# Attention into a gated MLP block: two casts ahead of the power on GpSimd, one cast later, a key turn moved, one output row to ScalarE, four stores to GpSimd's queue

## The chip, the core and the metric

The kernel runs on one core of one Trainium2 chip. The core has five engines that run their own instruction streams side by side and wait for each other through semaphores: TensorE (PE; its weight loads are listed apart as PEld), VectorE (DVE), ScalarE (ACT), GpSimd (POOL) and SyncE (SP), which here does nothing but start DMA transfers. ACT and POOL can start transfers as well; a letter q behind a name (SPq, POOLq) means the part of an engine that starts them. The metric is the device time of one execution in microseconds (us), as the median over several runs.

## What is computed

Attention over 4 batches, 8 heads, 768 positions and 64 features, in which each position sees the 128 latest positions and 4 "sink" positions at the start; then a block on the result `x` (768 x 512 for each batch):

```python
scores = scale * q @ k.T                       # kept where is_sink or in_window
a = exp(scores - max) / (sum + 1e-09)
x = (a @ v), heads side by side                # (4, 768, 512)

h = gelu_tanh(x @ w_in)                        # (768, 1024)
u, v = h[..., :512], h[..., 512:]
v_n = (v - mean(v)) / sqrt(var(v) + 1e-06) * g_ln
v_s = einsum('ts,bsd->btd', w_sg, v_n) + b_sg  # mixes positions
out = x + (u * v_s) @ w_out
```

## The kernel before

**Pairs.** Two heads of a batch are one pair `n`; batch b has the pairs 4b to 4b+3, so pairs 0 to 15 in all. "Pair 11" below is the pair with n = 11, the twelfth. For each pair:

- `load_all(n)` starts on SP the loads of k and q of pair n and of v of pair n-1; each kind has three buffers.
- `cast(n, which, G)` makes bf16 of them on POOL (L108 for k and q, L105 for v). k_bf and q_bf have two buffers each, v has four.
- `columns` turns k and q on PE, six 128x128 transposes into a PSUM bank (L221), and copies the result to SBUF on ACT (L225) or DVE (L227). `columns_by_dma` (L235) does it with two transposing DMAs on SP instead.
- `score(n, groups)` makes the scores of three groups (L269, L279) and takes the exponential on ACT (L283). `keep_band` puts zeros outside the window: group 0 on DVE (L292), groups 1 and 2 on POOL, two instructions each (L300, L302).
- `values(n, 0)` and `values(n, 1)` multiply with v (L326, L332) and divide on DVE (L334, L335) into `x_sb`. `turn_x` (L343, L352) or `turn_x_by_dma` (L356) turns x.

**Batches.** When four pairs are done, `hidden(b)` runs: six units `hidden_v` (L372, L379, gelu on ACT at L381, mean and variance on DVE at L383 and L384), eight units `hidden_u` (L391, L394). After the second of the latter comes `inverse_root`: `w`, variance plus epsilon, on DVE (L406), and its power -1/2, `y`, on POOL (L407). Then six `normalise` on DVE (L413), each reading fp32 from SBUF and writing bf16.

**Fillers.** The rest of a batch's work is put into a list of small units, which are mixed into the next batch's pairs so that PE always has something to do: eight `spatial` (six matmuls at L423, then two DVE instructions, L426 and L429) and six `project` (one for each 128 rows: four matmuls at L455). A row ends in one of two ways: DVE adds x to the PSUM bank and writes `o_sb` (L465), or PE adds x with one more matmul by the identity (L458) and ACT copies (L463). Then a store leaves (L467), on SP unless `store` says otherwise; `o_sb` has six buffers. The last row of the last batch goes in two halves (`project_last`, L440 to L447), one by DVE and SP, one by ACT and its own queue.

**Order.** Nothing is scheduled by a program: each engine's instructions stand in the order in which the text issues them, and an engine that waits holds up everything behind it in its own stream. The text of `ORDER` and `INSIDE` spells the order of steps for pairs 4 to 15. `S n g` is `score`, `m n g` is `keep_band`, `A0`/`A1` is `values`, `ck`/`cq`/`cv` are the casts on POOL, `KA`/`QA`/`QV` is `columns` with the copy on ACT or DVE, `TD` is `columns_by_dma`, `XV`/`XD` turns x, `L` is `load_all`, `F 1` takes one filler, `B b` runs `hidden(b)`. `INSIDE[b]` names steps between the units of `hidden(b)`: step i stands behind unit i, units 0 to 5 being `hidden_v` and 6 to 13 `hidden_u`; the power is issued behind unit 7.

**Limits on running ahead.** `bank` hands out four PSUM banks in turn to all of `columns`, `values`, `turn_x`, `hidden_*`, `spatial` and `project`, so PE can be at most four such units ahead of the engine that empties them; scores have two double banks of their own.

At the end of the kernel, the sixteen pairs' reciprocals are checked on POOL and PE, each engine reads the count, and a branch that is hardly ever taken follows.

Of the kernel before, what the change touches and what calls it, by code (L numbers as in the profile page):

```python
# [18 lines left out]
def kernel(  # L19
# [14 lines left out]
    nc = tc.nc  # L34
    V, G, A = nc.vector, nc.gpsimd, nc.scalar

    B, H, S, Dh = q.shape
# [10 lines left out]
    HT = NT // 2  # L48
# [162 lines left out]
    def bank(shape, dtype, name):  # L211
        return ps_m.tile(shape, dtype, name=name, tag="m")
# [162 lines left out]
    def hidden_v(b, j):  # L375
        if (b, j) not in hvs:
            open_v(b, j)
        h_ps, c = hvs.pop((b, j)), KD - 1
        nc.tensor.matmul(h_ps, xT[b][:, c, 128 * j:128 * (j + 1)],  # L379
                         w_in_sb[:, c, DF:], start=False, stop=True)  # L380
        A.activation(out=v_alls[b][:, j, :], in_=h_ps, func=AF.Gelu_apprx_tanh)  # L381
        st = small.tile([128, 6], F32, name="st")
        V.bn_stats(out=st, in_=v_alls[b][:, j, :])  # L383
        V.bn_aggr(out=mvs[b][:, j, :], in_=st)  # L384

    def hidden_u(b, f, n):
        if f == 0 and n == 0:
            uTs[b] = work.tile([128, KU, S], BF16, name="uT", bufs=1)
        h_ps = bank([128, 512], F32, "hu")
        for c in range(KD):  # L390
            nc.tensor.matmul(h_ps[:, 0:NH], w_in_sb[:, c, 128 * f:128 * (f + 1)],  # L391
                             xT[b][:, c, NH * n:NH * (n + 1)],
                             start=(c == 0), stop=(c == KD - 1))
        A.activation(out=uTs[b][:, f, NH * n:NH * (n + 1)],  # L394
                     in_=h_ps[:, 0:NH], func=AF.Gelu_apprx_tanh)
# [6 lines left out]
    def inverse_root(b):  # L402

        w = small.tile([128, NT], F32, name="w", bufs=2)
        y = small.tile([128, NT], F32, name="y", bufs=2)
        V.tensor_scalar(out=w, in0=mvs[b][:, :, 1], scalar1=1e-6, scalar2=None, op0=ALU.add)  # L406
        G.tensor_tensor(out=y, in0=w, in1=minus_half, op=ALU.pow)  # L407
        rstds[b] = y

    def normalise(b, j):  # L410
        if j == 0:
            vns[b] = work.tile([128, NT, DF], BF16, name="vn", bufs=1)
        V.tensor_scalar(out=vns[b][:, j, :], in0=v_alls[b][:, j, :],  # L413
                        scalar1=mvs[b][:, j, 0:1], scalar2=rstds[b][:, j:j + 1],
                        op0=ALU.subtract, op1=ALU.mult)

    def spatial(b, f, n):
        if f == 0 and n == 0:
            gTs[b] = work.tile([128, KU, S], BF16, name="gT", bufs=1)
        cols = slice(NH * n, NH * (n + 1))  # L420
        vs = bank([128, 512], F32, "vs")
        for si in range(NT):
            nc.tensor.matmul(vs[:, 0:NH], vns[b][:, si, 128 * f:128 * (f + 1)],  # L423
                             wsgT[:, si, cols], start=(si == 0), stop=(si == NT - 1))
        gv = small.tile([128, NH], BF16, name="gv")
        V.scalar_tensor_tensor(  # L426
            out=gv, in0=vs[:, 0:NH], scalar=g_sb[:, f:f + 1], in1=b_bc[:, cols],
            op0=ALU.mult, op1=ALU.add)
        V.tensor_mul(gTs[b][:, f, cols], gv, uTs[b][:, f, cols])  # L429
# [19 lines left out]
    def project(b, t, by_act, ends=None, store=nc.sync):  # L449

        rows = slice(128 * t, 128 * (t + 1))
        o_ps = bank([128, 512], F32, "o_ps")
        o_sb = small.tile([128, DM], F32, name="o_sb", bufs=6)
        for c in range(KU):
            nc.tensor.matmul(o_ps, gTs[b][:, c, rows], w_out_sb[:, c, :],  # L455
                             start=(c == 0), stop=(c == KU - 1 and not by_act))
        if by_act:
            nc.tensor.matmul(o_ps.rearrange("p (h d) -> p h d", h=HP), iden, x_sb[b][:, :, t, :],  # L458
                             start=False, stop=True)

        def end():
            if by_act:
                A.copy(o_sb, o_ps)  # L463
            else:
                V.tensor_add(o_sb.rearrange("p (h d) -> p h d", h=HP),  # L465
                             o_ps.rearrange("p (h d) -> p h d", h=HP), x_sb[b][:, :, t, :])
            store.dma_start(out=out[b, rows, :], in_=o_sb)  # L467

        if ends is None:
            end()  # L470
        else:
            ends.append(end)
# [107 lines left out]
    fillers = []  # L580
# [6 lines left out]
    def hidden(b, between):  # L587
        units = [lambda j=j: hidden_v(b, j) for j in range(NT)]
        units += [lambda f=f, n=n: hidden_u(b, f, n) for n in range(2) for f in range(KU)]
        after = {NT + 1: [lambda: inverse_root(b)]}  # L590
        for j in range(NT):
            after.setdefault(NT + 1 + j, []).append(lambda j=j: normalise(b, j))
        for i, unit in enumerate(units):
            unit()
            for step in after.get(i, []) + between.get(i, []):
                step()
        gate = [[lambda f=f, n=n: spatial(b, f, n) for f in range(KU)] for n in range(2)]
        if b < B - 1:
            fillers.extend(gate[0] + gate[1])
            by_act = (1,)  # L600
            order = (0, 2, 4, 1, 3, 5) if b < B - 2 else (1, 0, 2, 3, 4, 5)
            fillers.extend(lambda ends=None, t=t: project(b, t, t in by_act, ends) for t in order)
            return


        rows = [lambda t=t: project(b, t, t in (0, 4), store=nc.sync if t else G)
                for t in range(NT - 1)]
        fillers.extend(gate[0] + [gate[1][0], rows[0], gate[1][1], gate[1][2], rows[1],
                                  gate[1][3]] + rows[2:])
        fillers.append(lambda: project_last(b, NT - 1))  # L610
# [85 lines left out]
    for j in range(3):  # L696
# [15 lines left out]

    LAST = NT + 2 * KU - 1
    INSIDE = {
        1: {1: "A0 8", 3: "A1 8", 5: "KA 9", 6: "L 12", 7: "QA 9",
            9: "XD 8, ck 11, cq 11, TD 11, L 13", LAST: "cv 10, S 9 0 1, F 1, QV 10, F 1"},
        2: {1: "A0 12", 3: "A1 12", 6: "L 15, L 16", 9: "XD 12", LAST: "S 13 0 1, F 2"},
    }
    ORDER = """
        S 4 0 1, W 3 4 5, m 4 0 1, F 1, KA 5, QV 5, F 1, S 4 2, m 4 2, ck 6, cq 6, cv 5, F 1,  # L720
        L 8, S 5 0 1, A0 4, m 5 0 1, F 1, KA 6, S 5 2, m 5 2, A1 4, F 1, QA 6,
        ck 7, cq 7, cv 6, F 1, XV 4,
        L 9, S 6 0 1, A0 5, m 6 0 1, F 1, KA 7, S 6 2, m 6 2, A1 5, F 1, QA 7,
        ck 8, cq 8, cv 7, F 1, XV 5,
# [1 line left out]
        ck 9, cq 9, cv 8, F 1, XV 6,  # L726
        L 11, S 8 0 1, A0 7, m 8 1, D, S 8 2, m 8 2, A1 7, E, m 8 0, ck 10, cq 10, cv 9,
        O 1 0, O 1 1, XV 7, O 1 2, B 1,
        m 9 0 1, F 1, KA 10, F 1, S 9 2, m 9 2, ck 12, cq 12, TD 12, F 1,
        S 10 0 1, A0 9, m 10 0 1, F 1, S 10 2, m 10 2, A1 9, XD 9, L 14,  # L730
        F 1, cv 11, ck 13, cq 13, TD 13, F 1,
        S 11 0 1, A0 10, m 11 0 1, F 1, S 11 2, m 11 2, A1 10, F 1, cv 12, ck 14, cq 14, TD 14,
# [8 lines left out]
    ends = []  # L741
# [97 lines left out]
```

## Time and profile before

| | |
|---|---|
| median of 3 runs | 164.02 us (163.75 to 164.38) |
| the profiled execution, its own time | 164.03 us |
| its span in the trace | 162.0 us |
| DMA, mean over the span | 196 GB/s, 31.68 MB |
| stores of output rows on SP, 256 KB each | 22 |
| store of an output row on POOL | 1 |

The span runs from the first to the last instruction in the trace; some 2 us of the execution's own time lie outside of it. A row of the timeline gives start, length, engine, line, operation, what is written from what, how many instructions were merged, and in brackets how long the engine had been idle before and what released it. Consecutive matmuls overlap in the profile's model, so the start of the next one tells more about PE's pace than the length of one. In answers by stretches the columns are: the stretch, its length, busy time (and number of instructions) of each engine, the clock granted to PE, the DMA engines' share, and GB/s.

### The profile page before, as it was taken

The page shows a single profiled execution, that of the slowest core. Times are in us where ns is not written, and L with a number is a line of the kernel's source. Part 1 is how long each engine was busy: PE and PEld are TensorE (multiplying, and loading weights), DVE is VectorE, ACT ScalarE, POOL GpSimd, SP SyncE. Part 2 cuts the span into 40 slices and gives each one's busy share as a digit, 9 for nine tenths or more (in the row PEclk, how much of TensorE's full clock was granted, in tenths as well). Part 3 has the DMA queues.
Part 4 walks back from the last instruction along what each step waited for, and adds up shares of the span by engine and source line. Part 5 has one row for each costly group of instructions (what it writes and reads, how often), then busy time and mean ns, then how long its engine had stood idle before and what let it go on. Part 6 is the DMA issues. An engine that isn't in the chain of part 4 may idle for free.

```text
span 162.0 us, 4332 instructions
## 1 busy us (share of the span) xinstructions
PE 150.3 (93%) x1713; PEld 89.9 (55%) x1731; DVE 128.8 (79%) x279; ACT 103.0 (64%) x139; POOL 87.2 (54%) x121
## 2 busy tenths in 40 slices
PE   2999999999999999999899999999999899999940
PEld 2546574566667675565556655565566445555420
DVE  6786985966899995796999994969999957797820
ACT  3179978789777699788865576679659157401020
POOL 6567680434899989708449997031997221101000
PEclk9999999999999999999999999999999999999995
DMA  4999979999999999999897999999626420050352
GB/s 129 339 337 264 210 103 272 222 254 318 305 232 321 260 304 314 234 256 171 182 249 175 154 220 126 304 236 200 178 52 53 134 109 4 0 194 0 129 202 75
DMA packets 65090, 31.68 MB, mean 196 GB/s; under 512 B 53829, under 2 KB 62041, under 8 KB 65065
## 3 DMA queue, kind: packets, MB, share of 16 engines
q1 hardware_dynamic: 61616, 27.80, 74.8%
q0 software_dynamic: 3024, 3.03, 11.0%
q10 hardware_dynamic: 424, 0.53, 1.0%
q8 instruction: 15, 0.25, 0.7%
q14 instruction: 11, 0.08, 0.1%
HBM read 24.81 MB, written 6.29 MB: 192 GB/s over the span
## 4 chain that ended last, share of the span: by engine, by line
PE 45%; DVE 23%; issue 11%; POOL 10%; DMA 3%; ACT 3%; SPq 1%; POOLq 0%; ACTq 0%; DVEq 0%
PE vs L423 9%; PE hu L391 7%; PE o_ps L455 6%; PE hv L372 5%; DVE gv L426 4%; DVE gT L429 4%; DVE vn L413 4%; PE sc L269 3%; PE av L326 3%; DMA q_sb<-in_q_dram 3%; ACT ex L283 2%; DVE x L335 2%; POOL ex L300 2%; POOL ex L302 2%; PE kps L221 2%
## 5 line engine op out<-in xcount | busy, mean ns | idle before, releaser
L283 ACT ACTIVATE ex<-sc 128x1024 bf16<-128x1024 f32 x48 | 47.5, 1024 | 15.3 <-PE sc L269 6.4
L423 PE MATMUL vs<-wsgT,vn 128*128 128x384 bf16 x192 | 35.3, 326 | 0.5 <-DVE qT L227 0.4
L423 PEld LDWEIGHTS <-vn 128*128 128x128 bf16 x192 | 17.9, 98 | 11.3 <-issue 0.5
L300 POOL TENSOR_SCALAR_AFFINE_SELECT ex<-ex 128x512 bf16<-128x512 bf16 x24 | 18.6, 773 | 10.4 <-ACT ex L283 10.4
L455 PE MATMUL o_ps<-w_out_sb,gT 128*128 128x512 bf16 x83 | 22.2, 379 | 0.9 <-DVE x L335 0.4
L391 PE MATMUL hu<-xT,w_in_sb 128*128 128x384 bf16 x128 | 22.4, 326 | 0.0
L426 DVE SCALAR_TENSOR_TENSOR gv<-vs,g_sb,b_bc 128x384 bf16<-128x384 f32 x32 | 19.5, 610 | 2.1 <-PE vs L423 1.4
L381 ACT ACTIVATE v_all<-hv 128x512 f32<-128x512 f32 x24 | 13.3, 599 | 9.6 <-PE hv L379 8.4
L383 DVE BATCH_NORM_STATS2 st<-v_all 128x6 f32<-128x512 f32 x24 | 16.1, 670 | 3.5 <-ACT v_all L381 3.5
L335 DVE TENSOR_TENSOR x<-av,rcps 128x384 bf16<-128x384 f32 x32 | 17.8, 557 | 1.1
L372 PE MATMUL hv<-w_in_sb,xT 128*128 128x512 bf16 x68 | 18.4, 379 | 0.3
L394 ACT ACTIVATE uT<-hu 128x384 bf16<-128x384 f32 x32 | 15.7, 493 | 4.3 <-PE hu L391 3.8
L108 POOL CAST k_bf<-k_sb 128x768 bf16<-128x768 f32 x15 | 12.7, 845 | 10.3 <-DMA k_sb<-in_k_dram 10.3
L413 DVE TENSOR_SCALAR vn<-v_all,mv,y 128x512 bf16<-128x512 f32 x24 | 13.3, 619 | 5.9 <-POOL y L407 5.9
L429 DVE TENSOR_TENSOR gT<-gv,uT 128x384 bf16<-128x384 bf16 x32 | 15.5, 484 | 1.9
L108 POOL CAST q_bf<-q_sb 128x768 bf16<-128x768 f32 x15 | 14.7, 981 | 3.3 <-DMA q_sb<-in_q_dram 2.4
L391 PEld LDWEIGHTS <-w_in_sb 128*128 128x128 bf16 x128 | 12.1, 98 | 7.7
L269 PE MATMUL sc<-qT,kT 64*128 64x256 bf16 (+2 forms) x384 | 16.0, 256 | 0.4
L407 POOL TENSOR_TENSOR y<-w,minus_half 128x6 f32<-128x6 f32 x4 | 5.4, 1345 | 20.0 <-DVE w L406 20.0
L326 PE MATMUL av<-v_sb,ex 128*128 128x65 bf16 x352 | 16.1, 194 | 0.0
L326 PEld LDWEIGHTS <-ex 128*128 128x128 bf16 x352 | 13.0, 97 | 4.9 <-issue 1.7
L105 POOL CAST v_sb<-v_sb 128x768 bf16<-128x768 f32 x16 | 13.7, 855 | 3.4 <-DMA v_sb<-in_v_dram 3.3
(89 smaller groups left out, 216.5 us busy)
## 6 DMA issues: line engine op xcount, KB each, us to landing
k_sb<-in_k_dram SPq DMA_DIRECT2D x16, 384.0 KB, 6.9
v_sb<-in_v_dram SPq DMA_DIRECT2D x16, 384.0 KB, 6.4
q_sb<-in_q_dram SPq DMA_DIRECT2D x15, 384.0 KB, 6.9
out_dram<-o_sb SPq DMA_DIRECT2D x22, 256.0 KB, 2.6
wsg_sb<-in_moe_w_sg_dram POOLq DMA_DIRECT2D x2, 576.0 KB, 11.4
w_in_sb<-in_moe_w_in_dram POOLq DMA_DIRECT2D x2, 256.0 KB, 5.8
w_in_sb<-in_moe_w_in_dram POOLq DMA_DIRECT2D x1, 512.0 KB, 6.7
w_out_sb<-in_moe_w_out_dram POOLq DMA_DIRECT2D x1, 512.0 KB, 9.5
```

What stands on the lines that cost most here:

```text
L108: eng.tensor_copy(dst.rearrange("p t (h d) -> p h t d", h=2), src)
L269: nc.tensor.matmul(sc[part, 512 * l + w:512 * l + w + n_q], kT[rows, 128 * j + wide * a:128 * j + wide * (a + 1)], qT[rows, 128 * j:128 * ...
L283: A.activation(out=exps[n][:, g, :], in_=sc, func=AF.Exp, scale=scale)
L300: eng.affine_select(out=diag, in_=diag, compare_op=ALU.is_ge, fill=0.0, base=0, pattern=[[0, 2], [0, 2], [1, 128]], channel_multiplier=-1)
L326: nc.tensor.matmul(av[:, m, l, :], probs(j, l, half), v_sb[:, l, j, :], start=first, stop=False)
L335: V.tensor_mul(x_sb[b][:, hp, HT * c:HT * (c + 1), :].rearrange("p i (l d) -> p i l d", l=2), av[:, :, :, 0:64], rcp.to_broadcast([128, HT ...
L372: nc.tensor.matmul(hvs[b, j], xT[b][:, c, 128 * j:128 * (j + 1)], w_in_sb[:, c, DF:], start=(c == 0), stop=False)
L391: nc.tensor.matmul(h_ps[:, 0:NH], w_in_sb[:, c, 128 * f:128 * (f + 1)], xT[b][:, c, NH * n:NH * (n + 1)], start=(c == 0), stop=(c == KD - 1))
L423: nc.tensor.matmul(vs[:, 0:NH], vns[b][:, si, 128 * f:128 * (f + 1)], wsgT[:, si, cols], start=(si == 0), stop=(si == NT - 1))
L426: V.scalar_tensor_tensor(out=gv, in0=vs[:, 0:NH], scalar=g_sb[:, f:f + 1], in1=b_bc[:, cols], op0=ALU.mult, op1=ALU.add)
L429: V.tensor_mul(gTs[b][:, f, cols], gv, uTs[b][:, f, cols])
L455: nc.tensor.matmul(o_ps, gTs[b][:, c, rows], w_out_sb[:, c, :], start=(c == 0), stop=(c == KU - 1 and not by_act))
```

## The change

Four edits in the order of work; no instruction's work changes but for one output row that ends on another engine.

1. `ck 11` and `cq 11` move in `INSIDE[1]` from step 9 to step 6, which is ahead of the power (behind unit 7) in POOL's stream. `cv 10` moves from the end of `hidden(1)` into `ORDER`, behind `ck 12, cq 12`. `TD 11`, which reads the first two, stays at step 9.
2. `KA 6` moves behind `S 5 2, m 5 2`.
3. For the batch `B - 3`, which is batch 1, row 5 ends by ACT as row 1 does.
4. For the batch `B - 2`, which is batch 2, the last three rows in its order (3, 4 and 5) are stored by POOL; of the last batch row 3 (`HT`) is stored by POOL and row 0 by SP.

```diff
         if b < B - 1:
             fillers.extend(gate[0] + gate[1])
-            by_act = (1,)
+            by_act = (1, 5) if b == B - 3 else (1,)
             order = (0, 2, 4, 1, 3, 5) if b < B - 2 else (1, 0, 2, 3, 4, 5)
-            fillers.extend(lambda ends=None, t=t: project(b, t, t in by_act, ends) for t in order)
+
+            by_pool = () if b < B - 2 else order[-3:]
+            fillers.extend(lambda ends=None, t=t: project(b, t, t in by_act, ends,
+                                                          G if t in by_pool else nc.sync)
+                           for t in order)
             return
...
-        rows = [lambda t=t: project(b, t, t in (0, 4), store=nc.sync if t else G)
+        rows = [lambda t=t: project(b, t, t in (0, 4), store=G if t == HT else nc.sync)
                 for t in range(NT - 1)]
...
     INSIDE = {
-        1: {1: "A0 8", 3: "A1 8", 5: "KA 9", 6: "L 12", 7: "QA 9",
-            9: "XD 8, ck 11, cq 11, TD 11, L 13", LAST: "cv 10, S 9 0 1, F 1, QV 10, F 1"},
+        1: {1: "A0 8", 3: "A1 8", 5: "KA 9", 6: "L 12, ck 11, cq 11", 7: "QA 9",
+            9: "XD 8, TD 11, L 13", LAST: "S 9 0 1, F 1, QV 10, F 1"},
...
-        L 8, S 5 0 1, A0 4, m 5 0 1, F 1, KA 6, S 5 2, m 5 2, A1 4, F 1, QA 6,
+        L 8, S 5 0 1, A0 4, m 5 0 1, F 1, S 5 2, m 5 2, KA 6, A1 4, F 1, QA 6,
...
-        m 9 0 1, F 1, KA 10, F 1, S 9 2, m 9 2, ck 12, cq 12, TD 12, F 1,
+        m 9 0 1, F 1, KA 10, F 1, S 9 2, m 9 2, ck 12, cq 12, TD 12, cv 10, F 1,
```

## The prediction

> **What bounds the kernel now.** I read the page first (engines, chain), then the busy time by stretch, then the timeline of each engine round the places that the diff touches.
>
> ```profile
> span 162.0 us, 4332 instructions
> PE 150.3 (93%) x1713; PEld 89.9 (55%) x1731; DVE 128.8 (79%) x279; ACT 103.0 (64%) x139; POOL 87.2 (54%) x121
> ...
> PE 45%; DVE 23%; issue 11%; POOL 10%; DMA 3%; ACT 3%; SPq 1%; POOLq 0%; ACTq 0%; DVEq 0%
> ```
>
> TensorE (PE) is nearly always busy, so a stage gets shorter only where PE really waits. The chain nevertheless spends a third of its time on VectorE (DVE) and GpSimd (POOL): there are stretches in which PE keeps pace with DVE instead of running ahead. In the answer by stretches the second column is the length, and then come PE, PEld, DVE, ACT and POOL:
>
> ```profile
> 76.00:80.50 4.50, 4.08 (x33) 2.29 (x31) 4.50 (x8) 3.91 (x5) 2.10 (x4) 1.00 0.76 157
> 80.50:98.00 17.50, 17.33 (x262) 10.26 (x264) 17.01 (x38) 10.37 (x11) 15.18 (x21) 1.00 1.14 204
> ...
> 112.00:128.40 16.40, 15.91 (x227) 9.59 (x227) 15.95 (x35) 10.58 (x12) 11.00 (x15) 1.00 0.53 96
> ```
>
> From 76 to 80.5 DVE has no free moment (4.50 of 4.50) and PE does (4.08); from 112 to 128.4 DVE is as full as PE (15.95 and 15.91 of 16.40). Those two places can yield time. The granted clock (the column after POOL) is 1.00 in all of them, so it plays no part.
>
> **Part 1: the casts of pair 11 ahead of the power, the v cast of pair 10 later.** Around the second batch's power `y`:
>
> ```profile
> 71.55 0.50 PE L221 MATMUL qps<-iden,q_bf 128*128 128x128 bf16 x6
> ...
> 73.34 1.34 POOL L407 TENSOR_TENSOR y<-w,minus_half 128x6 f32<-128x6 f32 x1 [5.34 <-DVE w L406]
> ...
> 74.66 0.81 POOL L108 CAST k_bf<-k_sb 128x768 bf16<-128x768 f32 x1
> ...
> 76.39 1.02 POOL L105 CAST v_sb<-v_sb 128x768 bf16<-128x768 f32 x1
> ```
>
> POOL stands idle for 5.34 us before `y`, and then runs three casts from 74.66 to 77.41, exactly while DVE normalises (L413, six instructions). The same six instructions in the three batches (length, then DVE's busy time in them alone):
>
> ```profile
> 73.30:79.10 5.80, 4.33 (x6) 1.00 0.97 168
> 107.80:112.60 4.80, 3.31 (x6) 1.00 1.38 218
> 137.10:141.50 4.40, 2.88 (x6) 1.00 0.00 0
> ```
>
> Three casts beside them: 4.33 us; one cast (the third batch): 3.31; none: 2.88. That is 0.43 to 0.48 us of DVE per cast, and 1.45 us in all for batch 1. The change takes all three away from there.
>
> What do they cost where they go? The k and q casts (0.81 and up to 1.35, the longest cast quoted below) fall into the idle 5.34 us. The q cast overwrites one of two buffers, and in the new order it comes before the query turn of pair 9 in the text, so it must wait for that turn's transposes on PE (71.55 plus 0.50, 72.05). It then ends at 72.9 to 73.4, and `w` releases `y` at 73.34. So `y` keeps its place or slips by 0.1 at most; behind it in POOL's queue stand the masks of pair 9, which wait for ScalarE anyway. Nothing is lost even if `y` slipped by 1 us, since the normalisation behind it is 1.45 us shorter. The moved casts issue no DMA. Behind them on SP stand the two transposing DMAs of pair 11, which become free earlier, and the loads of pair 14, whose v buffer this cast now releases at 87 or so (behind the q cast of 85.26, quoted under B) instead of at 77.41; it is asked for at 91.51:
>
> ```profile
> 91.51 1.67 SPq L96 DMA_DIRECT2D v_sb<-in_v_dram  x1
> ```
>
>
> What does PE gain? At present:
>
> ```profile
> 78.50 1.14 PE L423 MATMUL vs<-wsgT,vn 128*128 128x384 bf16 x6
> ...
> 80.56 1.14 PE L423 MATMUL vs<-wsgT,vn 128*128 128x384 bf16 x6 [0.37 <-DVE qT L227]
> 81.63 0.36 PE L269 MATMUL sc<-qT,kT 64*32 64x256 bf16 x16
> ```
>
> The two units and the key turn between them take 81.63 - 78.50 = 3.13 us. Unhindered ones are in the next fence: a turn from 47.84 to 48.17 (0.33) and a unit from 48.17 to 49.15 (0.98). So 0.98 + 0.33 + 0.98 = 2.29, and PE loses 0.84 here to DVE's late normalisation and the copies queued behind it. With DVE 1.45 earlier all of that goes: **-0.85**. Its bounds are 0 (the wait returns further on, rival B) and -1.45 (DVE's whole lead, were DVE the only limit).
>
> **Part 2: pair 6's key turn behind the scores of pair 5, third group.**
>
> ```profile
> 44.34 1.14 PE L423 MATMUL vs<-wsgT,vn 128*128 128x384 bf16 x6
> 45.53 0.51 PE L221 MATMUL kps<-iden,k_bf 128*128 128x128 bf16 x6
> 45.97 0.36 PE L269 MATMUL sc<-qT,kT 64*32 64x256 bf16 x16
> ...
> 46.32 0.54 PE L326 MATMUL av<-v_sb,ex 128*128 128x65 bf16 x12
> ...
> 47.84 0.50 PE L221 MATMUL qps<-iden,q_bf 128*128 128x128 bf16 x6
> 48.17 1.14 PE L423 MATMUL vs<-wsgT,vn 128*128 128x384 bf16 x6
> 49.15 0.50 PE L343 MATMUL xps<-iden,x 128*128 128x128 bf16 x6
> ```
>
> The unit at 44.34 is through at 45.32; the turn starts at 45.53, waiting for POOL's cast. With the scores (0.35) first, the turn runs from 45.67 to 46.00, and `av` starts 0.32 earlier. On ScalarE the key copy now stands behind one more exponential (1.02 in the row of 114.55 below), and a unit that reuses the copy's bank comes just after it, so a little may be given back. I take **-0.25**, between 0 and -0.32.
>
> **Part 3: row 5 of the second batch ends on ScalarE.** DVE loses one of two additions, PE gains one identity matmul, ScalarE one copy.
>
> ```profile
> 112.43 1.27 DVE L465 TENSOR_TENSOR o_sb<-o_ps,x 128x512 f32<-128x512 f32 x2
> 113.64 1.16 POOL L300 TENSOR_SCALAR_AFFINE_SELECT ex<-ex 128x512 bf16<-128x512 bf16 x1 [3.70 <-ACT ex L283]
> 114.55 1.02 ACT L283 ACTIVATE ex<-sc 128x1024 bf16<-128x1024 f32 x1 [0.99 <-PE sc L279]
> ...
> 120.40 0.33 PEld L269 LDWEIGHTS <-kT 64*128 64x128 bf16 x8 [0.32 <-issue]
> ...
> 126.31 0.55 PEld L455 LDWEIGHTS <-gT 128*128 128x128 bf16 x4 [0.56 <-DVE x L335]
> ```
> ```profile
> 148.07 0.22 PE o_ps L458
> ```
>
> DVE is 1.27/2 = 0.63 us lighter at the start of the stretch in which it is full, and at the end of that stretch PE waits 0.56 for DVE. The wait goes; the extra matmul costs 0.22, partly inside time that PE spends on the normalisation anyway. The copy fits into ScalarE's idle 0.99. The row's store stands ahead of pair 15's transposes on SP and leaves about half a us later; pair 15's scores need them at 120.40. Net -0.56 + 0.22 = **-0.35**; bounds +0.22 and -0.56.
>
> **Part 4: the four stores on GpSimd's queue.** Rows 3, 4, 5 of the third batch leave while PE works on the last batch's gates; behind them SP and POOL only read the count for the branch at the very end. Row 0 of the last batch returns to SP. What matters is row 3 of the last batch. The first row is SP's issue just before its last one; the line of the DMA engines cuts 154 to 162 us into 40 slices; then the length of SP's 22 issues (min/median/max in ns) and, over all stores, the time from issue to landing, and the same for the one store that POOL issues now:
>
> ```profile
> 155.53 1.12 SPq L467 DMA_DIRECT2D out_dram<-o_sb  x1
> ```
> ```profile
> DMA  0009997989400102999989971110000000100000
> ```
> ```profile
> L467 SPq DMA_DIRECT2D out_dram<-o_sb x22: 332/373/1677, 56.9 to 155.5; - x22
> ...
> DMA to landing us min/median/max: 2.1/2.5/3.9
> ```
> ```profile
> DMA to landing us min/median/max: 2.4/2.4/2.4
> ```
>
> SP's last issue, the last half row, stands behind this one of 1.12 us. Were that as short as the shortest, 0.33, the last store could be issued 0.79 earlier, with row 3 out of SP's queue. But the DMA line says what the end waits for: after 158.6 only a tenth of the engines still works, and the slowest store needs 3.9 us against 2.1. One or two late DMA engines finish last, and moving row 3 to another queue does not take its bytes off them. POOL's landing of 2.4 keeps row 3 ahead of the last store. I take **0**, with -0.79 and +0.3 (2.4 against 2.1, if row 3 were last) as bounds. The Trainium skill says the same in "DMA: Bandwidth & Descriptors", section "Issuing engines are not separate DMA queues": DMAs from all engines run on the same 16 engines, and spreading them only saves issue time. By that rule at most the 0.79 could come.
>
> **The sum.** -0.85 - 0.25 - 0.35 + 0 = -1.45. The profiled execution took 164.03 us (span 162.0, 2.0 around it), the median of the runs is 164.02: 164.03 - 1.45 = 162.6.
>
> **The rivals.**
>
> Rival B: POOL becomes the bound. The v cast of pair 10 now stands in POOL's densest stretch (15.18 of 17.50), ahead of the masks of pairs 10 and 11:
>
> ```profile
> 85.26 1.35 POOL L108 CAST q_bf<-q_sb 128x768 bf16<-128x768 f32 x1
> ...
> 86.56 0.78 POOL L300 TENSOR_SCALAR_AFFINE_SELECT ex<-ex 128x512 bf16<-128x512 bf16 x1
> ...
> 88.52 0.36 PEld L326 LDWEIGHTS <-ex 128*128 128x128 bf16 x10 [0.21 <-issue]
> ...
> 91.94 0.78 POOL L300 TENSOR_SCALAR_AFFINE_SELECT ex<-ex 128x512 bf16<-128x512 bf16 x1
> ...
> 93.78 0.36 PEld L326 LDWEIGHTS <-ex 128*128 128x128 bf16 x10 [0.21 <-PE sc L269]
> ```
>
> `values` needs the first mask at 88.52; it is done at 87.34, slack 1.18; for pair 11 it is 93.78 - 92.72 = 1.06. POOL's stretch begins with a mask that follows PE, so it comes 0.85 earlier with PE. A cast of 0.81 leaves 0.25 to 0.37; one of 1.35, as beside DVE's two-input work, is 0.17 to 0.29 too long, and longer masks would take the rest of part 1. Then some 0.6 of the 0.85 is lost: 163.2 to 163.5, I say 163.4. Against it: DVE is earlier too, and both shift together.
>
> Rival C: the end gains as well. The late DMA engine is only late because SP's issue was held; then 0.79 comes on top: 161.8. For it: the 1.12 us. Against: the DMA line.
>
> Rival D, slower: POOL and DVE lengthen each other from 84 on. Its place is the masks between the new cast and pair 11's `values`. If four of these take the longest 1.16 us seen (row at 113.64) and not some 0.75, that adds 1.6, with the cast 0.95 and the lead 0.85: 92.72 + 1.6 + 0.95 - 0.85 = 94.4 against 93.8, so PE is 0.6 behind its old place; the extra matmul adds 0.2 and DVE, no longer ahead, keeps its wait at 126: 164.9. It decides from a cast plus lengthening of 2 us on. Against it: such masks are rare in that stretch.
>
> Rival E: it does not do what it says. PE's lead is absorbed by the next wait on DVE in each stretch, 0.3 in all remains: 163.8.
>
> **How the numbers follow.** Forecast 0.54 (162.6; its own range 162.0 to 163.2), B 0.15, C 0.13, D 0.10, E 0.08. About 0.5% (0.8 us) is what a measurement of this kernel can tell from no change; the bounds are 163.2 and 164.8. Faster: most of the forecast, all of C, a little of B: 0.67. Slower: most of D: 0.09. Between: 0.24. The range 161.6 to 164.1 leaves out D, and gains beyond C.
>
> **What would show it.** L413 of the second batch at 2.9 to 3.1 us; `y` after both casts with no delay past `w`; the wait for `qT` at 80.56 gone and the scores of pair 9 some 0.85 plus 0.25 earlier; `kps` of pair 6 with no wait for POOL's cast; the wait for `x` at 126 gone; the distance from the last matmul to the end as before. I am wrong if POOL's masks are what `values` waits for at 88 or 94 (B, D), if `y` starts later relative to `w`, or if the end after the last matmul changes by more than 0.3.

## The result and the profile after

| | before | after |
|---|---|---|
| median (lowest to highest) of 6 runs each | 164.19 us (163.75 to 164.62) | 162.38 us (161.98 to 163.05) |
| after / before | | 0.9894, 95% interval 0.9867 to 0.992 |
| the profiled execution, its own time | 164.03 us | 161.98 us |
| its span | 162.0 us | 160.1 us |
| own time less span | 2.03 us | 1.84 us |

Of every kernel some executions are slow ones, several per cent longer than the rest; the medians, ratios and traces below are of the others alone, so E6, whose profiled execution was slow, stands in no comparison of traces.

The page of the kernel after, the engines and the chain that ended last:

```profile
PE 150.5 (94%) x1732; PEld 89.8 (56%) x1732; DVE 128.0 (80%) x278; ACT 103.7 (65%) x140; POOL 87.3 (55%) x124
...
PE 73%; DMA 16%; SPq 4%; POOL 2%; DVE 1%; issue 1%; ACT 0%; POOLq 0%
```

The busy times hardly moved; the chain did. VectorE's share of it went from 23% to 1% and GpSimd's from 10% to 2%: TensorE now holds 73% of it, and DMA transfers hold 16%.

The stretches of the prediction, in the kernel after (stretch, length, then PE, PEld, DVE, ACT, POOL; the last one is moved forward, since TensorE is earlier there):

```profile
76.00:80.50 4.50, 4.50 (x38) 2.58 (x34) 4.50 (x9) 4.14 (x5) 0.88 (x1) 1.00 0.94 191
80.50:98.00 17.50, 17.50 (x264) 10.23 (x263) 16.53 (x35) 10.82 (x13) 16.36 (x24) 1.00 1.11 183
...
111.20:126.90 15.70, 15.70 (x227) 9.51 (x226) 15.25 (x33) 10.82 (x13) 9.80 (x15) 1.00 0.44 99
```

TensorE fills all three (4.50 of 4.50 where it had 4.08). VectorE still has no free moment from 76 to 80.5, but nobody waits for it there any more. The granted clock is 1.00 in all three, as before.

The six normalisations (L413) alone, in the three batches:

```profile
73.30:79.10 5.80, 2.83 (x6) 1.00 1.02 180
106.80:111.80 5.00, 3.30 (x6) 1.00 1.38 218
135.50:140.20 4.70, 2.88 (x6) 1.00 0.00 0
```

4.33 us became 2.83 in the second batch; the other two are as they were. GpSimd's timeline round the power:

```profile
70.36 0.83 POOL L108 CAST k_bf<-k_sb 128x768 bf16<-128x768 f32 x1 [2.55 <-issue]
71.99 0.83 POOL L108 CAST q_bf<-q_sb 128x768 bf16<-128x768 f32 x1 [0.81 <-PE qps L221]
73.16 1.35 POOL L407 TENSOR_TENSOR y<-w,minus_half 128x6 f32<-128x6 f32 x1 [0.34 <-DVE w L406]
```

The bracket behind `q_bf` is the wait for the query turn's transposes that the prediction named; the one behind `y` says that GpSimd was idle when `w` came, so `y` is not held by the casts.

TensorE's timeline of the kernel after, at the moved key turn and behind the normalisation:

```profile
44.59 1.14 PE L423 MATMUL vs<-wsgT,vn 128*128 128x384 bf16 x6
45.66 0.36 PE L269 MATMUL sc<-qT,kT 64*32 64x256 bf16 x16
...
46.01 0.51 PE L221 MATMUL kps<-iden,k_bf 128*128 128x128 bf16 x6
...
47.86 0.50 PE L221 MATMUL qps<-iden,q_bf 128*128 128x128 bf16 x6
...
78.32 1.14 PE L423 MATMUL vs<-wsgT,vn 128*128 128x384 bf16 x6
79.29 0.50 PE L221 MATMUL kps<-iden,k_bf 128*128 128x128 bf16 x6
79.63 1.14 PE L423 MATMUL vs<-wsgT,vn 128*128 128x384 bf16 x6
80.69 0.36 PE L269 MATMUL sc<-qT,kT 64*32 64x256 bf16 x16
```

An absolute start also carries what happened earlier, so intervals are compared. From the unit ahead of pair 6's key turn to the query turn behind it: 47.86 - 44.59 = 3.27, where before it was 47.84 - 44.34 = 3.50: 0.23 less. From the unit at 78.32 to the scores of pair 9: 2.37, where it was 3.13: 0.76 less, and the wait for `qT` in brackets is gone.

TensorE's weight loads where VectorE's `x` held it at 126 us, after and then before:

```profile
124.31 0.56 PEld L326 LDWEIGHTS <-ex 128*128 128x128 bf16 x10
...
124.86 0.56 PEld L455 LDWEIGHTS <-gT 128*128 128x128 bf16 x4
```
```profile
125.13 0.56 PEld L326 LDWEIGHTS <-ex 128*128 128x128 bf16 x10
```

0.55 us lie between them now; before it was 126.31 (the row in the prediction) less 125.13, 1.18: 0.63 less.

GpSimd's dense stretch and the weight loads of the two `values` that need its first masks, in the kernel after:

```profile
85.47 0.97 POOL L105 CAST v_sb<-v_sb 128x768 bf16<-128x768 f32 x1
86.40 0.63 POOL L300 TENSOR_SCALAR_AFFINE_SELECT ex<-ex 128x512 bf16<-128x512 bf16 x1
...
91.77 0.63 POOL L300 TENSOR_SCALAR_AFFINE_SELECT ex<-ex 128x512 bf16<-128x512 bf16 x1
```
```profile
87.59 0.36 PEld L326 LDWEIGHTS <-ex 128*128 128x128 bf16 x10 [0.21 <-issue]
...
92.74 0.36 PEld L326 LDWEIGHTS <-ex 128*128 128x128 bf16 x10 [0.21 <-PE sc L269]
```

The masks are done at 87.03 and 92.40, with 0.56 and 0.34 us to spare: the slack of 1.18 and 1.06 has shrunk, but holds.

**The end.** The last copy on ScalarE, before and after:

```profile
155.90 0.37 ACT L446 COPY o_last<-o_ps 128x256 f32<-128x256 f32 x1 [0.40 <-PE o_ps L445]
```
```profile
154.46 0.37 ACT L446 COPY o_last<-o_ps 128x256 f32<-128x256 f32 x1 [0.40 <-PE o_ps L445]
```

It comes 1.44 us earlier, which is the predicted sum. The span is 1.86 us shorter (162.00 against 160.14 in the trace) and the own time 2.05. So 0.42 us were won between that copy and the end of the span, and 0.19 outside of it. The prediction had nothing for either, and most of the experiments are about them.

### The profile page after: what moved, and what is told of

Read it like the earlier page. It is cut to its first block, busy times and chain, and to the rows that moved or that the text cites. A ratio compares the mean times of both kernels' runs of the same rounds, so it can differ in the third digit from the quotient of the medians.

```text
span 160.1 us, 4355 instructions
## 1 busy us (share of the span) xinstructions
PE 150.5 (94%) x1732; PEld 89.8 (56%) x1732; DVE 128.0 (80%) x278; ACT 103.7 (65%) x140; POOL 87.3 (55%) x124
## 4 chain that ended last, share of the span: by engine, by line
PE 73%; DMA 16%; SPq 4%; POOL 2%; DVE 1%; issue 1%; ACT 0%; POOLq 0%
PE vs L423 19%; PE o_ps L455 13%; PE hu L391 10%; DMA wsg_sb<-in_moe_w_sg_dram 8%; PE hv L372 7%; PE sc L269 6%; PE av L326 6%; DMA v_sb<-in_v_dram 4%; SPq L96 4%; DMA k_sb<-in_k_dram 4%; PE hv L379 2%; PE av L332 2%; PE xps L343 1%; PE kps L221 1%; PE qps L221 1%; PE wps L203 1%
## 5 line engine op out<-in xcount | busy, mean ns | idle before, releaser
L300 POOL TENSOR_SCALAR_AFFINE_SELECT ex<-ex 128x512 bf16<-128x512 bf16 x24 | 16.9, 706 | 13.5 <-ACT ex L283 13.1
L413 DVE TENSOR_SCALAR vn<-v_all,mv,y 128x512 bf16<-128x512 f32 x24 | 11.8, 559 | 5.9 <-POOL y L407 5.9
L108 POOL CAST q_bf<-q_sb 128x768 bf16<-128x768 f32 x15 | 13.8, 919 | 4.6 <-PE hu L391 2.3
L105 POOL CAST v_sb<-v_sb 128x768 bf16<-128x768 f32 x16 | 14.2, 886 | 3.5 <-DMA v_sb<-in_v_dram 3.5
L302 POOL TENSOR_SCALAR_AFFINE_SELECT ex<-ex 128x512 bf16<-128x512 bf16 (+1 forms) x24 | 13.8, 577 | 0.0
```

What stands on the lines that cost most here:

```text
L108: eng.tensor_copy(dst.rearrange("p t (h d) -> p h t d", h=2), src)
L300: eng.affine_select(out=diag, in_=diag, compare_op=ALU.is_ge, fill=0.0, base=0, pattern=[[0, 2], [0, 2], [1, 128]], channel_multiplier=-1)
```

## The experiments

E1 to E4 each make one part of the change alone, on the kernel before. The others are edits of the changed kernel.

**E1, the casts alone.**

```diff
-        1: {1: "A0 8", 3: "A1 8", 5: "KA 9", 6: "L 12", 7: "QA 9",
-            9: "XD 8, ck 11, cq 11, TD 11, L 13", LAST: "cv 10, S 9 0 1, F 1, QV 10, F 1"},
+        1: {1: "A0 8", 3: "A1 8", 5: "KA 9", 6: "L 12, ck 11, cq 11", 7: "QA 9",
+            9: "XD 8, TD 11, L 13", LAST: "S 9 0 1, F 1, QV 10, F 1"},
...
-        m 9 0 1, F 1, KA 10, F 1, S 9 2, m 9 2, ck 12, cq 12, TD 12, F 1,
+        m 9 0 1, F 1, KA 10, F 1, S 9 2, m 9 2, ck 12, cq 12, TD 12, cv 10, F 1,
```

> Before plus the moved casts alone. Theory (the casts beside DVE's normalisation made it long, PE gained what it had waited for it): L413 of the second batch 2.8 to 3.0 us, PE's start of pair 9's third score group 0.7 to 0.9 us earlier, and that lead kept until the third batch's hidden; PE's wait for DVE at 126 stays or grows, since DVE there is as full as before: 0.99 to 0.997 of before, 162.8 to 163.6 us. Rival (POOL's masks become the bound in the stretch behind): the lead shrinks to under 0.3 us at 94, ratio 0.997 to 1.002.

163.34 us against 164.37, ratio 0.9945 (0.9919 to 0.997). The answer for L413 alone, and TensorE's timeline:

```profile
73.30:79.10 5.80, 2.83 (x6) 1.00 1.09 182
```
```profile
78.50 1.14 PE L423 MATMUL vs<-wsgT,vn 128*128 128x384 bf16 x6
...
80.88 0.34 PE L269 MATMUL sc<-qT,kT 64*32 64x256 bf16 x10
```

2.38 us from the first unit to the scores, against 3.13: part 1 is worth 0.75 at this place by itself. The lead is kept: the last copy on ScalarE starts at 155.07 here, 0.83 earlier than in the kernel before.

**E2, the key turn alone.**

```diff
-        L 8, S 5 0 1, A0 4, m 5 0 1, F 1, KA 6, S 5 2, m 5 2, A1 4, F 1, QA 6,
+        L 8, S 5 0 1, A0 4, m 5 0 1, F 1, S 5 2, m 5 2, KA 6, A1 4, F 1, QA 6,
```

> Before plus the moved key turn alone. Theory: PE's values of pair 4, second half, 0.25 to 0.35 us earlier, still there at 70 and at the second batch's power; behind it the lead is kept only as far as DVE's normalisation follows PE: 0.2 to 0.35 us in all, ratio 0.998. Rival (the next wait for DVE or for the key's bank takes it back): 0 at 56, ratio 1.000.

164.23 us, ratio 0.999 (0.9969 to 1.0011), which is no change that the timing can tell. The timeline can:

```profile
44.21 1.14 PE L423 MATMUL vs<-wsgT,vn 128*128 128x384 bf16 x6
...
47.48 0.50 PE L221 MATMUL qps<-iden,q_bf 128*128 128x128 bf16 x6
```

3.27 us, as in the changed kernel, against 3.50. Both readings agree: 0.23 us is 0.14% of the time, inside the interval.

**E3, row 5 alone.**

```diff
-            by_act = (1,)
+            by_act = (1, 5) if b == B - 3 else (1,)
```

> Before plus row 5 of the second batch on ScalarE alone. Theory: PE 0.1 to 0.25 us later at 112 (one more matmul), the wait of 0.56 us at 126 gone, net 0.3 to 0.5 us earlier behind 127: ratio 0.9975. Rival (the wait at 126 has another cause than DVE's backlog): the wait stays and the kernel is 0.2 us slower.

163.97 us, ratio 0.9979 (0.9963 to 0.9995). TensorE's weight loads:

```profile
125.15 0.56 PEld L326 LDWEIGHTS <-ex 128*128 128x128 bf16 x10
...
125.70 0.56 PEld L455 LDWEIGHTS <-gT 128*128 128x128 bf16 x4
```

0.55 us instead of 1.18: the wait for `x` is gone with this part alone.

**E4, the stores alone.**

```diff
-            fillers.extend(lambda ends=None, t=t: project(b, t, t in by_act, ends) for t in order)
+            by_pool = () if b < B - 2 else order[-3:]
+            fillers.extend(lambda ends=None, t=t: project(b, t, t in by_act, ends,
+                                                          G if t in by_pool else nc.sync)
+                           for t in order)
...
-        rows = [lambda t=t: project(b, t, t in (0, 4), store=nc.sync if t else G)
+        rows = [lambda t=t: project(b, t, t in (0, 4), store=G if t == HT else nc.sync)
```

> Before plus the four stores on the other queue alone. All up to the last matmul within 0.05 us of before. Theory of the prediction (one late DMA engine sets the end): from the start of the last ScalarE copy to the end of the span 6.1 us as before, ratio 1.000. Rival (SP's held issue sets it): SP's last issue 0.7 to 0.8 us nearer to the last matmul and the end 0.4 to 0.8 us earlier, ratio 0.995 to 0.9975.

163.68 us, ratio 0.9958 (0.9937 to 0.9979): a gain of 0.69 us that the prediction had at nothing. In its profile the last copy starts at 155.88, within 0.02 us of the kernel before, so none of it lies ahead of the end. The ratio lies where the rival (SP's held issue) had put it, but from the last copy to the end of the span it is 5.86 us against 6.11, only 0.25 less where that rival had 0.4 to 0.8; another 0.22 lies outside the span (1.81 against 2.03). The four ratios together lose 0.0055 + 0.001 + 0.0021 + 0.0042 = 0.0128; the whole change loses 0.0106 (0.008 to 0.0133). Within these intervals the parts add up.

**E5 to E7 and the changed kernel again.** E5 puts the v cast of pair 10 ahead of the power as well. E6 is the changed kernel without part 4. E7 keeps only the last batch's half of part 4: row 3 on GpSimd, row 0 on SP.

```diff
-        1: {1: "A0 8", 3: "A1 8", 5: "KA 9", 6: "L 12, ck 11, cq 11", 7: "QA 9",
+        1: {1: "A0 8", 3: "A1 8", 5: "KA 9", 6: "L 12, ck 11, cv 10, cq 11", 7: "QA 9",
...
-        m 9 0 1, F 1, KA 10, F 1, S 9 2, m 9 2, ck 12, cq 12, TD 12, cv 10, F 1,
+        m 9 0 1, F 1, KA 10, F 1, S 9 2, m 9 2, ck 12, cq 12, TD 12, F 1,
```
```diff
-            fillers.extend(lambda ends=None, t=t: project(b, t, t in by_act, ends,
-                                                          G if t in by_pool else nc.sync)
-                           for t in order)
+            fillers.extend(lambda ends=None, t=t: project(b, t, t in by_act, ends) for t in order)
```

(The second diff is E7; E6 also turns `rows` back.)

> The changed kernel once more, as the measure for the three beside it. Median 0.987 to 0.992 of the kernel before (it was 0.9894). If the shorter tail of its first profile (5.64 us from the start of the last ScalarE copy to the end, against 6.10 before) is the stores' work it comes again at 5.6 to 5.8; if it was chance in when one late DMA lands, it can come out at 6.0 to 6.4 too.

> The changed kernel with the stores on their old queues; parts 1 to 3 remain. Theory (the stores are worth what they gave alone, 0.42%): 0.9935 of the kernel before, 0.004 slower than the changed kernel; the last issue on SP again starts or ends over 1.0 us behind the start of the last copy on ScalarE, against 0.5. Rival (the stores are worth nothing, as the prediction had it): 0.9895, the same as the changed kernel within 0.0015.

> The changed kernel with the three rows of the third batch stored by SP again; only row 3 of the last batch by GpSimd and row 0 by SP remain of part 4. Theory (what counts is SP's issue just ahead of its last one): the same as the changed kernel, 0.9894, and SP's last issue is done 0.5 to 0.9 us behind the start of the last copy. Rival (the three rows of the third batch count, since they crowd SP or the DMA engines ahead of the end): the same as without part 4, some 0.9935.

> The changed kernel with the v cast of pair 10 also ahead of the power (between the k and the q cast of pair 11) instead of behind pair 12's. Theory (GpSimd's dense stretch still has slack, TensorE does not wait for it): the same as the changed kernel within 0.15%, 0.988 to 0.991; normalise of the second batch stays at 2.8 to 2.9 us, and the last q cast, and with it y, is not late by more than 0.2 us since GpSimd had 2.55 and 0.81 us idle there. Rival (the v cast lengthens the masks there and these hold TensorE a little): 0.3 to 0.5% faster than the changed kernel, 0.985 to 0.9865.

| kernel | median | ratio to before (interval) |
|---|---|---|
| the changed kernel again | 162.28 | 0.987 (0.9833 to 0.9907) |
| E5, v cast early too | 162.46 | 0.9865 (0.9836 to 0.9895) |
| E6, without part 4 | 163.03 | 0.9915 (0.9887 to 0.9942) |
| E7, the last batch's half of part 4 | 162.84 | 0.9902 (0.9873 to 0.9931) |

The changed kernel's tail, from the last copy to the end of its span, is 5.41 us in this second profile, shorter than either of its theories had it. Tails scatter with the last landing: 5.41 to 6.08 us in the traces with part 4 whole, 6.10 to 6.58 in those of before, E1 to E3 and E7.

E5 is as fast as the changed kernel measured beside it: whether this one cast stands ahead of the power or in the dense stretch does not matter, and GpSimd still has slack there, as the theory said. E6 and E7 are slower than the changed kernel by 0.45% and 0.32%, the size of E4's gain, but the intervals overlap, and E6's holds both of its theories (0.9935 and 0.9895). E7's theory fell in its trace: its tail from the last copy to the end is 6.10 us, that of the kernel before, although row 3 is out of SP's way. So the gain hangs on the three rows of the third batch, which are issued at 140.9 to 142.6 us, some 18 us before the end.

**Where the gain of part 4 lies.** Behind the branch at the very end SP reads its eight semaphores of hardware DMAs one after another. The groups of the line that holds the branch (L803 before, L807 after) show these eight looks with the first and the last start, in the kernel before and after:

```profile
L803 SPq EVENT_SEMAPHORE  x8: 17/17/17, 159.4 to 160.3; - x8
```
```profile
L807 SPq EVENT_SEMAPHORE  x8: 17/17/17, 155.5 to 158.0; - x8
```

By the trace's records of the transfers the last store is down at 159.30 before and 157.50 after. Before, all eight looks come behind that, one every 0.07 to 0.09 us once the first two have got through; after, six are done ahead of it and only two are left. The records of the looks name the semaphores. These are the starts, in us behind the start of the last copy, by the number of the semaphore:

```
semaphore      99    101   111   112   113   114   115   116
before        3.50  3.94  4.03  4.12  4.19  4.26  4.33  4.40
after         1.04  1.14  1.22  1.31  1.55  2.89  3.22  3.52
```

The two half rows that leave last hold 101 (SP) and 111 (ScalarE) before. The second look is the one that waits, and six follow it: 4.40 - 3.94 = 0.46 us. After, they hold 115 and 116, the last two, and nothing follows. The semaphores go round the DMAs of SP and ScalarE in turn; three fewer of them in the third batch turn the round by three.

The other piece lies outside the span. The DMA view of the last 5 us, cut into 40 slices of 0.125 us, before (159.5 to 164.5) and after (157.6 to 162.6):

```profile
DMA  0000000000010000000000000000000000200000
...
q14 instruction: 2, 0.02, 1.1%
```
```profile
DMA  0000100000000000010000000000000000000000
...
q14 instruction: 2, 0.02, 0.8%
```

Queue q14 fetches instructions, 8 KB at a time, and nothing else moves here. So the lone tenth at 160.8 us in the prediction's DMA line is an instruction fetch. The tenths at 158.8 and 159.0 are still packets of stores and nothing else, as the DMA view from 158.8 to 159.2 of the kernel before says; the one at 159.2 holds both.

```profile
q1 hardware_dynamic: 13, 0.01, 11.4%
q10 hardware_dynamic: 3, 0.00, 1.6%
```

What the prediction missed is that the span goes on for 2.70 us after the last store is down. Before, the last fetch stands in slice 34 (counted from 0), at 163.8, which is 1.8 us behind the end of the span; after, the last is at 159.8, ahead of the end at 160.1.

**E10 and E13, the two pieces apart.** E10 sends the three rows by ScalarE's queue. E13 leaves them on SP and stores five rows of the third batch in two halves each, so that the round turns by five more, which is three fewer modulo eight.

```diff
-                                                          G if t in by_pool else nc.sync)
+                                                          nc.scalar if t in by_pool else nc.sync)
```
```diff
-            store.dma_start(out=out[b, rows, :], in_=o_sb)
+            if b == B - 2 and t != 1:
+                for h in range(2):
+                    cols = slice(256 * h, 256 * (h + 1))
+                    store.dma_start(out=out[b, rows, cols], in_=o_sb[:, cols])
+            else:
+                store.dma_start(out=out[b, rows, :], in_=o_sb)
```

> The changed kernel with the three rows of the third batch stored by ScalarE's queue instead of GpSimd's; SP's stream is as short as in the changed kernel. Theory: the gain of part 4 inside the span comes from the order in which SP looks at its eight semaphores of hardware DMAs at the end. These go round all DMAs of SP and ScalarE, three fewer of them in the changed kernel put the last store on the last ones looked at, and six looks of 0.07 to 0.09 us behind the binding one fall away (0.45 us). Stores on ScalarE count in the same round, so this gain should be gone: some 2.6 us or more from the last landing to the end of the span as before, and 0.99 of the kernel before. The 0.2 us outside the span should stay won (own time less span 1.75 rather than 1.97) if the instruction fetch behind the end is SP's, and be lost if it is GpSimd's. Rival (what counts is SP's own issues, which are no longer in the way): as the changed kernel, 0.987 to 0.9895, on both counts.

> The changed kernel with no row of the third batch on GpSimd's queue, and five of that batch's rows stored by SP in two halves each: five more hardware DMAs, which moves the round of eight semaphores as three fewer do. Theory (the order of SP's looks): the 0.45 us inside the span is won although SP has eight issues more than in the changed kernel; last landing to the end of the span 2.1 to 2.3 us; own time less span stays at 1.97, since SP's stream is longer; 0.988 to 0.989 of the kernel before. Rival (fewer issues on SP win it): as the kernel with only the last batch's store moved, 0.990 or slower, 2.6 us.

E10: 162.44 us, ratio 0.9876 (0.9844 to 0.9907). E13: 162.59 us, ratio 0.9892 (0.9863 to 0.9921). The times do not separate the theories: both intervals hold 0.990, and E10's middle lies on the rival's side. The ends of the traces do. The looks of E10 and of E13:

```profile
L807 SPq EVENT_SEMAPHORE  x8: 17/17/17, 158.2 to 159.4; - x8
```
```profile
L808 SPq EVENT_SEMAPHORE  x8: 17/17/17, 156.1 to 158.6; - x8
```

And the last 5 us of their DMA engines, E10 (158.6 to 163.6, its span ends at 161.1) and E13 (157.8 to 162.8, 160.3):

```profile
DMA  0002000000000000000000000000000000200000
```
```profile
DMA  0002000000000002000000000000000000200000
```

The profiled executions that can be compared, by their traces (us; the last two columns against the end of the span):

| kernel | last copy to last landing | looks left at the landing | landing to last look | landing to end of span | own time less span | last fetch |
|---|---|---|---|---|---|---|
| before | 3.41 | 8 | 0.99 | 2.70 | 2.03 | +1.81 |
| E1 | 3.67 | 7 | 1.20 | 2.91 | 2.03 | +1.80 |
| E2 | 3.70 | 7 | 0.95 | 2.66 | 2.01 | +1.81 |
| E3 | 3.44 | 8 | 1.04 | 2.74 | 1.97 | +1.81 |
| E7 | 3.50 | 7 | 0.89 | 2.60 | 2.01 | +1.82 |
| E10, rows by ScalarE | 3.71 | 7 | 0.90 | 2.61 | 2.02 | +1.81 |
| E13, ten halves on SP | 3.55 | 2 | 0.49 | 2.20 | 2.06 | +1.80 |
| after | 3.04 | 2 | 0.49 | 2.64 | 1.84 | -0.38 |
| after, again | 3.27 | 2 | 0.43 | 2.14 | 1.72 | -0.83 |
| E4 | 3.62 | 2 | 0.52 | 2.23 | 1.81 | -0.53 |
| E5 | 3.85 | 2 | 0.52 | 2.24 | 1.73 | -1.81 |
| E12 | 3.67 | 2 | 0.54 | 2.26 | 1.72 | -1.17 |
| E8 | 3.52 | 2 | 0.52 | 2.24 | 1.84 | -1.12 |

Two effects, and each goes with its own cause. The landing to the last look is 0.43 to 0.54 us wherever the round is turned, by three rows on GpSimd or by five halves more, and 0.89 to 1.20 elsewhere; E13 has the gain with eight more issues on SP than the changed kernel, and E10 lacks it with as few as the changed kernel. The late fetch is gone exactly where GpSimd got three more stores: not in E10, whose SP stream is as short, and not in E13. Over all runs of the first kind that are compared (37 of six kernels) the own time less the span has a median of 1.75 us, over those of the second (49 of seven) 1.98: 0.23 us. Single runs overlap (1.67 to 1.88 and 1.71 to 2.09). What is shown is that the late fetch and the 0.23 us go together with the three stores on GpSimd's queue; whose instructions that fetch brings, and why these stores move it ahead of the end, is not.

**E12, one cast back beside the normalisation.**

```diff
-            9: "XD 8, TD 11, L 13", LAST: "S 9 0 1, F 1, QV 10, F 1"},
+            9: "XD 8, TD 11, L 13", LAST: "cv 10, S 9 0 1, F 1, QV 10, F 1"},
...
-        m 9 0 1, F 1, KA 10, F 1, S 9 2, m 9 2, ck 12, cq 12, TD 12, cv 10, F 1,
+        m 9 0 1, F 1, KA 10, F 1, S 9 2, m 9 2, ck 12, cq 12, TD 12, F 1,
```

> The changed kernel with the v cast of pair 10 at its old place, beside the second batch's normalise; the k and q casts stay ahead of the power. Normalise rises from 2.83 to 3.2 to 3.4 us (0.43 to 0.48 for one cast). Theory (VectorE is 1.45 us earlier with all three casts gone, TensorE needs only some 0.8 of it): the 0.45 is covered, TensorE at the scores of pair 9 and the time are as in the changed kernel within 0.15 us. Rival (each cast costs TensorE a third of the gain): 0.25 us or more later from there on, 0.16% slower than the changed kernel.

162.16 us, ratio 0.9865 (0.984 to 0.989). L413 alone, GpSimd's cast and TensorE's timeline:

```profile
73.80:79.60 5.80, 3.31 (x6) 1.00 0.97 177
```
```profile
75.02 0.81 POOL L105 CAST v_sb<-v_sb 128x768 bf16<-128x768 f32 x1
```
```profile
78.86 1.14 PE L423 MATMUL vs<-wsgT,vn 128*128 128x384 bf16 x6
...
81.24 0.36 PE L269 MATMUL sc<-qT,kT 64*32 64x256 bf16 x16
```

One cast costs VectorE 0.48 us (3.31 against 2.83) and TensorE nothing up to the scores: 2.38 us, as with none. But the shorter lead shows at the next place where TensorE waits for VectorE's `x`, at 92 us. These are TensorE's weight loads there, in E12 and in the changed kernel:

```profile
91.29 0.69 PEld L455 LDWEIGHTS <-gT 128*128 128x128 bf16 x4
...
92.88 0.33 PEld L269 LDWEIGHTS <-kT 64*128 64x128 bf16 x8
```
```profile
90.75 0.69 PEld L455 LDWEIGHTS <-gT 128*128 128x128 bf16 x4
...
92.20 0.33 PEld L269 LDWEIGHTS <-kT 64*128 64x128 bf16 x8
```

From the row's projection to the next scores it takes 1.59 us in E12 and 1.45 in the changed kernel; before it was 1.56 (91.68 to 93.24). The theory held within its 0.15 us, which the time cannot tell from nothing: two of the three casts carry the gain at the two units, and the third is worth 0.14 at 92 us.

**E8, row 3 on ScalarE too.**

```diff
-            by_act = (1, 5) if b == B - 3 else (1,)
+            by_act = (1, 3, 5) if b == B - 3 else (1,)
```

> The changed kernel with row 3 of the second batch ended by ScalarE too. Theory (with row 5 alone TensorE no longer waits at the fourth batch's first projections, so there is nothing left to win and one more identity matmul of 0.22 us to pay): 0.2 us slower than the changed kernel by TensorE's timeline. Rival (VectorE still holds TensorE in that stretch): the same or up to 0.4 us faster.

162.54 us, ratio 0.9889 (0.986 to 0.9918): not faster. By TensorE's timeline against the changed kernel it loses 0.22 us at the added identity matmul (110.29) and wins nothing behind it, as the theory had it. No version was found that beats the changed kernel.

## Why the prediction was right, and where it was not

| step | predicted | in the profiles |
|---|---|---|
| part 1, the casts | -0.85 | -0.76 at 79 to 81 us (E1: -0.75), -0.11 at 92 us (E1: the same) |
| part 2, the key turn | -0.25 | -0.23 (E2: -0.23) |
| part 3, row 5 | -0.56 + 0.22 = -0.35 | -0.63 at the wait (E3: -0.63), +0.24 for the matmul |
| what is left, up to the last copy | 0 | +0.05 |
| **up to the last copy** | **-1.45** | **-1.44** (155.90 to 154.46) |
| part 4, the stores | 0 | -0.42 in the span, -0.19 outside (E4 by its time: -0.69) |
| **own time** | **-1.45** | **-2.05** (median -1.81) |

- **Part 1** was right in its mechanism and its size. The normalisation lost the whole 1.45 us foreseen (1.50), the two units and the turn came to 2.37 instead of the 2.29 worked out. `y` started at 73.16 instead of 73.34 and waited for `w` alone. E12 adds what the prediction did not say: at the two units TensorE needs only some 0.8 of VectorE's 1.50 us of lead, and a little of the rest is used at 92 us (1.56 became 1.45).
- **Part 2** was right: `kps` has no wait, and 0.23 of the 0.25 was kept up to the query turn.
- **Part 3** was right: the wait at 126 is gone, a little more than its bracket of 0.56 said, and the matmul cost its 0.22 to 0.24. E8 shows the limit of the argument: with the wait gone the next row brings only the cost.
- What is left is the difference of two shifts that nobody foresaw: TensorE is 0.26 us later at the transposes at 36 us, ahead of which nothing was changed (see the last section), and it gets 0.20 back at a wait for `x` at 55 us, of which E1, E3 and E4, unchanged there, get 0.15 too. That the sum was met to 0.01 us is luck; its three terms are not.
- **Part 4 is the step that failed**: "One or two late DMA engines finish last, and moving row 3 to another queue does not take its bytes off them", with 0 as its price. For row 3 this held: E7, which moves it alone, has the tail of the kernel before. But the sum ended at the last transfer and looked at row 3 alone. The last store was down at 159.30, and 2.70 us more followed: SP's looks at its semaphores, the end of the program and, outside the span, an instruction fetch. The three rows of the third batch changed what follows, by 0.46 us in the looks and 0.23 outside the span. Neither was in the sum, nor among the rivals. The bound of -0.79 is as large as that, but it stood for SP's held issue, and the first column of the table of the profiled executions refutes this one: the last landing follows the last copy by 3.41 to 3.71 us without part 4's three rows on GpSimd and by 3.04 to 3.85 with them. The Trainium skill's rule in "DMA: Bandwidth & Descriptors", section "Issuing engines are not separate DMA queues", that another queue saves only the time of issuing, agrees with these rows as far as the transfers go; what was won here lies behind them.
- The sign "the distance from the last matmul to the end as before", wrong beyond 0.3, was missed: 0.42. In that one execution of the changed kernel the looks gave less than they do elsewhere (2.64 us from the landing to the end, against 2.14 to 2.26 in its five relatives), because ScalarE read its own semaphore only at 159.16, 1.17 us behind SP's last look, and a later read of SP took 0.47 us instead of 0.03; the landing happened to be early instead.
- **Rival B** (GpSimd becomes the bound) did not come about: 0.56 and 0.34 us of slack remained, and E5, with the cast taken out of that stretch again, is no faster. **Rival D** needed longer masks there; they took 0.63 to 0.75 us. **Rival C** had the right place and nearly the right size (161.8 against 161.98 for the profiled execution) with the wrong cause. **Rival E** is excluded by E1 and E3.
- Two readings in the prediction are a little off, without effect on its forecast: -0.56 + 0.22 is -0.34, and the DMA line falls to a tenth at 158.8 us, not at 158.6.

The predicted 162.6 us against a median of 162.38 is closer than its parts deserve, which is luck: the missing 0.6 us of part 4 stands against medians that lie a little above the profiled executions.

## What to carry to other kernels

Compare intervals between two matmuls around an edit rather than absolute starts: they gave each part to 0.1 us where timing alone could not tell 0.23 us from nothing. When an engine is full over a stretch, look for what another engine does beside it; two casts moved into an idle gap were worth more here than the addition taken off VectorE. Read the last microseconds record by record before pricing an edit there: a semaphore's place in a fixed order of looks and an instruction fetch decided some 0.7 us that no transfer explains, and three DMAs fewer, or five more, some 18 us ahead of the end turned that order.

## What the runs showed of the hardware

- A GpSimd cast of 0.81 us beside VectorE's six normalisations lengthened them by 0.48 us (E12), three casts by 1.50. All of that is in the instructions that start while a cast runs. They take 1.02 to 1.04 us each, the others 0.52 to 0.55. The one in E12, beside the cast at 75.02:

```profile
75.09 1.03 DVE L413 TENSOR_SCALAR vn<-v_all,mv,y 128x512 bf16<-128x512 f32 x1 [1.47 <-POOL y L407]
```

  By the records the cast ends at 75.84 and this instruction at 76.12, and in all such pairs of before, after, E1, E3, E8 and E12 the instruction ends 0.28 to 0.29 us behind the cast. The Trainium skill describes the port pair that both share ("SBUF — State Buffer", section "SBUF: two separate sides") as an exclusive lock that stops the other engine for a whole instruction; the trace agrees in that none of these instructions finishes before the cast beside which it started. By that rule an estimate of the loss would be up to the cast's full 0.81; it is less here, since some 0.26 of the instruction's own 0.54 us passes while the cast runs.
- A look at a semaphore that is already up costs SP 0.07 to 0.09 us, so that six of them are 0.46 us of the kernel when they come last.
- An instruction fetch that starts 1.8 us behind the last recorded instruction goes with 0.23 us of execution time outside the span (medians of 1.98 and 1.75).
- TensorE's start on the transposes at L203 depends on when a load lands. The timeline of the changed kernel's second run:

```profile
36.72 1.01 PE L203 MATMUL wps<-iden,wsg_sb 128*128 128x128 bf16 x15 [0.64 <-DMA wsg_sb<-in_moe_w_sg_dram]
```

  By the records of the traces the same step went on at 36.33 us in its first run and at 36.03 in the kernel before, where nothing ahead of it was changed: single executions differ by some tenths from there, which is why parts of 0.2 us were read from intervals.
